# Attention, mixture of experts and FFN in one kernel: the products with v in plain float32, two heads side by side on TensorE's columns

## The chip, the cores and the metric

The kernel runs on one NeuronCore of one Trainium2 chip. The metric is the device time of one execution in microseconds (us). TensorE (PE) multiplies matrices and writes PSUM banks; VectorE (DVE), ScalarE (ACT) and GpSimd (POOL) do the elementwise work; the queue of SyncE (SP) starts nearly all DMA transfers. PSUM has eight banks here, each a tile of 128 partitions by 512 float32.

## The reference, cut to what matters

Three blocks follow one another on 4 batches of 448 rows. The first is causal attention with 12 heads of width 64, the second a layer of 4 experts, each of which is causal attention with one head of width 64 on the output of the first block, and the third an FFN with a convolution of three taps and a gate.

```
scores = scale * q @ k.T ; scores = where(mask, -1e9, scores)
attn = exp(scores - max) ; attn = attn / (sum(attn) + 1e-9)
x = attn @ v                                  # 12 heads, joined to 768 columns
for e in range(4):                            # experts: top 2 of 4 by x @ w_gate
    a = softmax(causal(scale * (x @ wq[e]) @ (x @ wk[e]).T))
    out += weight[e] * (a @ (x @ wv[e]) @ wo[e])
h = relu(out @ w_in) ; g = h * sigmoid(conv3(h)) ; y = g @ w_out
```

Everything is float32.

## The kernel before

Two heads make a pair. There are 24 pairs of attention (kind A, six for each batch) and 8 pairs of experts (kind M, two for each batch), so 64 heads. One head goes through these steps, each of which is a task with an engine:

- `score(i)`: PE, for four blocks of 112 rows (`CP`), two matmuls each. Operands are float32 numbers that have been split into a high and a low part of type float32r (`hi`, `lo`), so that a product is a sum of products of parts.
- `rowmax(i)` on DVE adds the mask and takes the maximum; `soft(i)` on ACT takes the exponential and the sum; `total`, `recip` on DVE; `norm(i)`, mostly on POOL, scales the rows of P.
- `transpose(g)`: PE turns P in three groups (448, 336 and 336 columns) into one of the two banks of kind `t`.
- `evac_hi(g)` copies a group out of the bank into `PT[:, 0]` as float32r (ACT; the six pairs of batch 0 are `plain`, and there ACT or DVE copies plain float32). `evac_lo(g)`, not for plain pairs, is a subtraction on DVE that reads the bank again and leaves the low part in `PT[:, 1]`. The bank is free after the last of the two.
- `pv(kts)`: PE multiplies with v. For a pair that isn't plain a head has two matmuls (high and low part of P) for each of four blocks of keys, 448, 336, 224 and 112 columns wide, against the weights `vhl[:, kt, 2h:2h+2]`, which hold the high part of v in 64 columns and the low part in the other 64. The two halves of the result are added by `out_corr` (ACT moves one half to `corr`) and `out_add` (DVE). For attention `x_hi` and `x_lo` on POOL then split x for the projections. For a plain pair a head has one float32 matmul for each block, with 64 columns of zeros beside v, and both heads sum into one bank, from which `pair_hi` and `pair_lo` split x at once.
- `v_hi`, `v_lo` on POOL split v of attention, `hi` and `lo` in `proj_v` that of the experts.

After a batch of attention come the projections `proj_qk` and `proj_v` for the experts; `fold_all` multiplies two weight matrices in the first 100 us. When all attention is done, `ffn_batch` and `ffn_out` do the FFN, with 1189 and 1257 as the lines of their matmuls.

No order is written out. `Program.run` is a planner: it walks through the program by a table of costs, and whenever an engine is idle it gives it the ready task of least priority number. The numbers are the table `PR` with one entry for each kind of task, `slot` for each pair. `ON` names the engines that may do a task. A task waits until the rings (`RINGS`, numbers of buffers) and the banks (`BANKS`) that it takes are free. Where the planner sees PE idle for more than 700 ns it puts in matmuls of `ident` with `ident` (`warm`, line 1334), whose results nobody reads. The order that it finds is fixed in the program; on the chip the engines only wait for each other.

Of the kernel before, what the change touches and what calls it, by code (L numbers as in the profile page):

```python
# [228 lines left out]
def attn_moe_ffn_kernel(  # L229
# [36 lines left out]
        P=3, PT=2, corr=2, x=2, nat=1, vn=1, skA=2, vhl=2, vw=2, skM=1, vhlm=1, wg=2,  # L266
# [4 lines left out]
        load=(-4152.0, 11493.0, -1929.0, 5893.5), prep=(-8501.0, 606.5, 168.5, 1518.0),  # L271
        vprep=(4890.5, 5076.0, 7982.5, 3170.0), wproj=-17.5, fold0=-467.0, fold=668.5,
        qk0=(-10900.5, -1866.5, -3202.0, 5747.5), v=(-554.5, -1155.5, -1893.5, 6792.5),
        qk1=(4984.5, 10288.0, 5857.0, 19987.0), evac=-3899.0, conv=-3380.0,
        wo=(-773.0, 5888.0, 4809.0, 9654.5, 9915.0, -4676.5), ffn0=-468.5,
        ffn=(5269.5, -4888.0, -1095.5, 4301.5), out=(2595.5, -1563.5, 2796.0, 1162.5),
        score=(2666.5, -704.5, 997.0, 78.5), rmax=(1169.5, 6674.0, 10054.0, -6359.0),
        exp=(2561.5, 12273.0, 3900.0, 4812.0), norm=(904.0, -404.5, -7099.5, 3076.5),
        tr=(4788.5, -3723.5, -5228.5, 1482.5), ev=(2394.5, 3956.5, -11469.5, -4991.0),
        pv=(5059.0, 512.0, -387.5, -3863.0), add=(-16794.0, 5422.5, -5662.5, -4891.0),  # L280
        x=(-1686.0, -6739.0, 4964.5, -45.5),
        slot=(-7300.5, -2095.0, -90.5, -898.5, 1247.5, 448.0, -4323.5, -2977.5, -2425.5, -1965.0, -9667.5, -1739.0, -466.5, -5300.0, 186.0, 145.5, -187.5, -146.5, 3848.5, 1960.5, 2151.5, -2484.5, 3906.0, 4302.5, 2325.0, 2446.5, 5199.0, 4478.5, 6267.0, 8256.0, 5325.5, -2013.5),
        other=(915.5, 3925.5, -1195.0, 6291.5, 8511.0, -4886.0, 7267.5, -2114.0, 1707.0, 15001.0, -10618.5, -9762.0, 1518.0, -1739.0, 5427.0, -14433.5, -6126.0),
        rows=(1435.0, 3384.5),
    )
    ON = dict(
        ql=('P', 'P', 'P', 'P'), norm=('PA', 'P', 'P', 'PD'), evp=('AD', 'A', 'A', 'A'), x_hi=('AP', 'P', 'P', 'P'),
        x_lo=('P', 'P', 'P', 'P'), v_hi=('P', 'P', 'P', 'P'), v_lo=('P', 'P', 'P', 'P'),
        q_hi=('DAP', 'A', 'A', 'A'), corr=('AD', 'A', 'A', 'A'), ev=('AD', 'A', 'A', 'A'),
        osb=('A', 'D', 'DA', 'A'),  # L290
    )
    KINDS = tuple(ON)
# [16 lines left out]
    def f(ap):  # L309
        return ap.bitcast(F32)  # L310
# [125 lines left out]
    for n, j in enumerate(order):  # L436
        j.slot = 8 * n
        j.slot += PR["slot"][n]
        j.plain = j.kind == "A" and j.b == 0
        j.phase = (0 if j.b == 0 else 1) if j.kind == "A" else 3 if j.b == B - 1 else 2  # L440
# [45 lines left out]
    def prep_twice(j):  # L486

        ready = {}
        for h in (1, 0):
# [3 lines left out]
            def load(h=h, st=st):  # L493
                if h == 1:
                    alloc_sk(j)
                t = pools["a"].tile([P, 2, TRI], F32, tag="PT", name=f"nat{h}", bufs=RINGS["PT"])
                st["nat"] = t[:, :, :S]
# [22 lines left out]
    def prep(j):  # L520
        n = f"{j.b}_{j.p}"
        nat, vn = Buf("nat"), Buf("vn")
        j.skb, j.vb = Buf("skA"), Buf("vhl")
# [5 lines left out]
        def load_v():  # L529
            j.v_nat = pools["head"].tile([CP, NQ, 2, D], F32, tag="vn", name=f"vn_{n}", bufs=1)  # L530
            nc.sync.dma_start(j.v_nat, v[j.b, j.p])
# [8 lines left out]

        def zero():
            j.vhl = pools["head"].tile([CP, NQ, 4, D], F32R, tag="vhl", name=f"vhl_{n}", bufs=RINGS["vhl"])
            nc.gpsimd.memset(f(j.vhl[:, :, 1, :]), 0.0)

        def load_v_apart():
            for h in range(2):
                nc.sync.dma_start(f(j.vhl[:, :, 2 * h]), v[j.b, j.p, :, :, h])
# [851 lines left out]
```

## Time and profile before

| | |
|---|---|
| time, median of 3 | 575.79 us (575.44 to 576.03) |
| the profiled execution | 573.99 us, of which its span is 572.2 us |
| PE busy | 94% of the span |
| DVE, ACT, POOL busy | 72%, 69%, 52% |
| mean granted TensorE clock | 0.979 of full speed |

The span goes from the first to the last instruction. A row of the profile names the line of the kernel, the engine, the operation, and the output and inputs by the program's names. A float32r matmul is one record; a plain float32 matmul is two (line 700 has 48 instructions and 96 records, line 1334 has 93 and 186).

### The profile page before, as it was taken

Reading aid. Unit: us, or ns where it says so; the run is one execution under the profiler, and the core shown is the slowest. Engines: PE = TensorE matmul, PEld = TensorE weight load, DVE = VectorE, ACT = ScalarE, POOL = GpSimd, SP = SyncE. Lnnn points to the kernel's source line nnn. Section 1 sums busy time; section 2 is a strip of 40 time slices with the busy share of each in tenths; the row PEclk is TensorE's granted clock in tenths of the full one; section 3 lists DMA queues with packets and bytes.
Section 4 is the critical chain, followed back from the end, with each engine's and each line's share of the span. In section 5 each row is a group of like instructions: output and inputs, shape, how many; then the busy total and the mean of one; then the engine's idle time right before and its main releaser. Section 6 shows DMA issues by size and latency. Waiting matters only on the chain.

```text
span 572.2 us, 10496 instructions
## 1 busy us (share of the span) xinstructions
PE 536.3 (94%) x3338; PEld 483.9 (85%) x3338; DVE 409.7 (72%) x1201; ACT 393.4 (69%) x1030; POOL 298.0 (52%) x466
## 2 busy tenths in 40 slices
PE   7979998899999999999989999978899999999997
PEld 7768787788988989888889999967798999889996
DVE  4879897785886888879867896588989962990000
ACT  3878768785896988989877996458758623881111
POOL 3465668686867779989679963444161330000000
PEclk8999999989999999999999999997999999999999
DMA  9998995787247376585665342161122131001111
GB/s 252 239 220 208 242 223 130 189 220 177 83 118 182 92 174 170 139 193 123 151 153 134 89 111 74 38 145 38 39 89 78 64 103 48 18 17 49 48 49 48
DMA packets 33287, 70.92 MB, mean 124 GB/s; under 512 B 9904, under 2 KB 18224, under 8 KB 33232
## 3 DMA queue, kind: packets, MB, share of 16 engines
q1 hardware_dynamic: 32944, 69.80, 47.9%
q10 hardware_dynamic: 288, 0.46, 0.3%
q8 instruction: 26, 0.43, 0.3%
q14 instruction: 29, 0.24, 0.1%
HBM read 32.74 MB, written 5.51 MB: 67 GB/s over the span
## 4 chain that ended last, share of the span: by engine, by line
PE 56%; DVE 19%; ACT 9%; DMA 8%; issue 4%; POOL 3%; SPq 1%; DVEq 0%; ACTq 0%; POOLq 0%
PE bank L1257 16%; PE bank L613 8%; PE bank L965 7%; PE bank L709 7%; PE bank L663 7%; PE bank L1011 5%; DVE bank L1210 4%; DMA sk_A<-sk_A 3%; PE bank L1189 2%; DMA nat<-in_qk_dram 2%; PE bank L700 2%; DVE PT_A L683 2%; DVE P_A L626 2%; ACT P_A L635 2%; ACT PT_A L319 1%
## 5 line engine op out<-in xcount | busy, mean ns | idle before, releaser
L1257 PE MATMUL bank<-g,wout 128*128 128x448 f32 x576 | 120.5, 367 | 0.0
L1257 PEld LDWEIGHTS bank<-g,wout 128*128 128x128 f32 x576 | 108.0, 188 | 9.7
L321 POOL TENSOR_SCALAR P_A<-P_A,r_A 112x448 f32<-112x448 f32 (+3 forms) x181 | 91.1, 518 | 37.5 <-DVE r_A L646 26.8
L635 ACT ACTIVATE P_A<-P_A,nm_A 112x448 f32<-112x448 f32 x192 | 100.2, 525 | 13.3 <-DVE nm_A L626 11.0
L613 PE MATMUL bank<-sk_A 128*112 128x112 f32 (+3 forms) x384 | 82.8, 326 | 10.7 <-DMA sk_A<-sk_A 5.7
L626 DVE CUSTOM_DVE_ANT_0 P_A<-bank,mask 112x448 f32<-112x448 f32 x192 | 81.7, 443 | 13.2 <-PE bank L613 12.1
L613 PEld LDWEIGHTS bank<-sk_A 128*112 128x112 f32 x384 | 57.3, 181 | 21.4 <-DVE nm_A L626 6.8
L663 PE MATMUL bank<-ident,P_A 112*112 112x112 f32 x480 | 66.7, 264 | 8.1 <-DVE PT_A L683 5.3
L965 PE MATMUL bank<-xT,wqk 128*128 128x448 f32 x288 | 73.5, 377 | 0.3 <-DVE wqk L941 0.2
L683 DVE TENSOR_TENSOR PT_A<-bank,PT_A 112x336 fp32r<-112x336 f32 (+1 forms) x108 | 57.9, 542 | 16.8 <-ACT PT_A L319 15.2
L319 ACT ACTIVATE PT_A<-bank 112x336 fp32r<-112x336 f32 (+2 forms) x128 | 59.5, 474 | 7.9 <-PE bank L663 6.9
L663 PEld LDWEIGHTS bank<-ident,P_A 112*112 112x112 f32 x480 | 49.5, 134 | 17.8 <-DVE PT_A L683 10.3
L328 POOL TENSOR_TENSOR sk_A<-nat,sk_A 128x896 fp32r<-128x896 f32 x23 | 48.5, 2109 | 19.5 <-ACT sk_A L319 12.0
L965 PEld LDWEIGHTS bank<-xT,wqk 128*128 128x128 f32 x288 | 49.7, 189 | 3.6 <-DVE wqk L941 1.0
L1189 PE MATMUL bank<-ocs,wp 128*128 128x448 f32 x192 | 45.8, 386 | 4.3 <-DVE g L1227 4.3
L709 PE MATMUL bank<-PT_A,vhl 112*128 112x448 f32 (+3 forms) x288 | 49.4, 316 | 0.0
L1210 DVE SCALAR_TENSOR_TENSOR bank<-h,cw,bank 128x448 f32<-128x448 f32 x64 | 43.0, 688 | 6.4 <-ACT bank L1208 5.7
L709 PEld LDWEIGHTS bank<-PT_A,vhl 112*128 112x128 f32 x288 | 46.2, 197 | 1.5
L1189 PEld LDWEIGHTS bank<-ocs,wp 128*128 128x128 f32 x192 | 37.1, 199 | 10.2 <-DVE g L1227 6.6
L319 ACT ACTIVATE osb<-bank 128x448 f32<-128x448 f32 x18 | 9.8, 545 | 47.1 <-PE bank L1257 47.0
L1011 PE MATMUL bank<-wvg,xT 128*112 128x260 f32 x288 | 41.4, 286 | 0.7 <-DVE sk_M L981 0.7
L321 POOL TENSOR_SCALAR P_M<-P_M,r_M,g_w 112x336 f32<-112x336 f32 (+3 forms) x60 | 34.1, 580 | 6.3 <-DVE r_M L646 4.8
(115 smaller groups left out, 1021.8 us busy)
## 6 DMA issues: line engine op xcount, KB each, us to landing
nat<-in_qk_dram SPq DMA_DIRECT2D x23, 448.0 KB, 5.1
sk_A<-sk_A SPq DMA_DIRECT2D x46, 224.0 KB, 4.3
sk_A<-sk_A SPq DMA_DIRECT2D x23, 336.0 KB, 3.4
wraw<-in_w_in_dram SPq DMA_DIRECT2D x12, 512.0 KB, 6.0
woraw<-in_w_out_dram SPq DMA_DIRECT2D x12, 512.0 KB, 3.8
out_dram<-osb SPq DMA_DIRECT2D x24, 224.0 KB, 1.9
sk_A<-sk_A SPq DMA_DIRECT2D x46, 112.0 KB, 4.0
vn<-in_v_dram SPq DMA_DIRECT2D x18, 224.0 KB, 4.0
```

The costliest lines, as they stand in the source:

```text
L319: nc.scalar.activation(dst, src, AF.Copy, scale=scale)
L321: nc.gpsimd.tensor_scalar(dst, src, scale, 1.0 if scale2 is None else scale2, ALU.mult, ALU.mult)
L613: nc.tensor.matmul(sp[:CP, :w], t[:, 1 - h, i * CP : (i + 1) * CP], t[:, 1 - h + k, :w], start=(k == 2), stop=(k == 1),)
L626: nc.vector.tensor_tensor_reduce(rows(i), st["s", i][:CP, :w], mask[:, S - w :], -SCALE, 3.0e38, ALU.add, ALU.min, st["nm"][:, i : i + 1],)
L635: nc.scalar.activation(rows(i), rows(i), AF.Exp, bias=st["nm"][:, i : i + 1], scale=-1.0, accum_out=st["sm"][:, i, 0:1],)
L663: nc.tensor.transpose(pt[:CP, o : o + CP], rows(i)[:, kt * CP : (kt + 1) * CP], ident[:CP, :CP])
L683: nc.vector.tensor_tensor(st["PT"][:, 1, b0 : b0 + w], pt, f(st["PT"][:, 0, b0 : b0 + w]), ALU.subtract)
L709: nc.tensor.matmul(st["ov"][:, kt * CP : S], j.vhl[:, kt, 2 * h : 2 * h + 2, :], st["PT"][:, s, col_base[kt] : col_base[kt] + w], start=(k ...
L965: nc.tensor.matmul(st["ps"][:, :S], proj["wqk"][:, a, cc, w, p * P : (p + 1) * P], xT[b, cc][:, b2, :], start=(cc == 0 and (a, b2) == PASS ...
L1011: nc.tensor.matmul(st[i][:CP, :VW], xT[b, cc][:, a, i * CP : (i + 1) * CP], proj["wvg"][:, b2, cc, :], start=(cc == 0 and (a, b2) == PASSE ...
L1189: nc.tensor.matmul(st["ps", c][:, :S], wp[:, a, ec, c * P : (c + 1) * P], st["oc"][:, b2, ec], start=(ec == 0 and (a, b2) == PASSES[0]), s ...
L1257: nc.tensor.matmul(st["ps"][:, :S], ffn["wout", n][:, a, c], gs[c][:, b2], start=(c == 0 and (a, b2) == PASSES[0]), stop=(c == NFC - 1 and ...
```

## The change

- v stays float32. It is loaded as it is (`load_v`, one DMA for each pair, in a ring of three), and the tasks `v_hi`, `v_lo`, `zero`, `load_v_apart` and the `lo` of `proj_v` are gone.
- P keeps no parts. `evac(g)` is one copy out of the bank, by ACT or DVE. The ring `PT` has four buffers of half the size, one for each head.
- `products_v` takes the place of `pv`, `out_corr`, `out_add`, `x_hi` and `x_lo`: when all six groups of a pair are copied, eight float32 matmuls with 64 columns of weights follow one another, head 1 and head 0 in turn. Head 1 writes partitions 64 to 127 of a bank, head 0 partitions 0 to 63. In the built program these are set as 128 by 64 tiles of the array at column 64 and column 0; all other matmuls are set as 128 by 128. An expert pair is then copied to `oc` at once, an attention pair is split from the bank into x (ACT or DVE, then DVE).
- FFN results have a ring of their own (`osb`, 4), and `oc` is split into two buffers, one for each pair of experts.
- The numbers in `PR` and the choices in `ON` are other ones.

```diff
-        PT=2, corr=2, x=2, nat=1, vn=1, skA=2, vhl=2, vhlm=1, ...
+        PT=4, osb=4, nat=1, skA=2, vn=3, vm=1, ...
-        score=(2666.5, -704.5, 997.0, 78.5), rmax=(1169.5, 6674.0, 10054.0, -6359.0),
+        score=(8996.0, -638.0, 1743.0, -7812.5), rmax=(-1352.5, 6783.0, 22485.0, -7290.0),
...
-        def evac_lo(g):
-            def go():
-                pt, b0, w = st["pt", g]
-                nc.vector.tensor_tensor(st["PT"][:, 1, b0 : b0 + w], pt, f(st["PT"][:, 0, b0 : b0 + w]), ALU.subtract)
...
-                    for s in range(2):
-                        nc.tensor.matmul(
-                            st["ov"][:, kt * CP : S],
-                            j.vhl[:, kt, 2 * h : 2 * h + 2, :],
-                            st["PT"][:, s, col_base[kt] : col_base[kt] + w],
...
+        cost = sum(2 * ((S - kt * CP) / 1.2 + PVX) for kt in range(NQ))
+        def pv():
+            st["ov"] = ps(vb)
+            for kt in range(NQ):
+                for h in (1, 0):
+                    nc.tensor.matmul(
+                        st["ov"][h * D : (h + 1) * D, kt * CP : S],
+                        j.v[:, kt, h, :],
+                        j.PT[h][:, col_base[kt] : col_base[kt] + S - kt * CP],
+                        start=(kt == 0),
+                        stop=(kt == NQ - 1),
+                    )
+        t = add("PE", prio + PR["pv"][j.phase], cost, pv, j.evs + j.vready, take=[vb], free=[j.PTb[1], j.PTb[0], j.vb])
...
+        def x_hi(e):
+            x = xT[(j.b, j.p)] = pools["x"].tile([P, 2, S], F32R, tag="xT", name=f"xT_{j.b}_{j.p}", bufs=RINGS["xT"])
+            copy(e, x[:, 0], st["ov"][:, :S])
+        def x_lo():
+            x = xT[(j.b, j.p)]
+            nc.vector.tensor_tensor(x[:, 1], st["ov"][:, :S], f(x[:, 0]), ALU.subtract)
```

The places in the order that matter are three. In the rows below a name carries the pair, the head and a running number (`PT_M_0_1_1867` is P transposed of the expert pair 0, head 1; since the change a further digit says whose head it is).

PE before, about two fifths into the attention: the products of two heads of an expert pair, scores of an attention pair between them.

```order
L709 MATMUL bank_65<-PT_M_0_1_1867,vhlm_1634 128x448 x2
L709 MATMUL bank_65<-PT_M_0_1_1867,vhlm_1634 128x336 x2
L709 MATMUL bank_65<-PT_M_0_1_1867,vhlm_1634 128x224 x2
L709 MATMUL bank_65<-PT_M_0_1_1867,vhlm_1634 128x112 x2
L613 MATMUL bank_62<-sk_A_4_1462 112x336 x2
L613 MATMUL bank_61<-sk_A_4_1462 112x224 x2
L709 MATMUL bank_66<-PT_M_0_0_1921,vhlm_1634 128x448 x2
```

PE of the change, the same pair.

```order
L581 MATMUL bank_61<-sk_A_4_1747 112x448 x2
L695 MATMUL bank_66<-PT_M_0_1_1_1884,vm_1579 64x448
L695 MATMUL bank_66<-PT_M_0_1_0_1885,vm_1579 64x448
L695 MATMUL bank_66<-PT_M_0_1_1_1884,vm_1579 64x336
L695 MATMUL bank_66<-PT_M_0_1_0_1885,vm_1579 64x336
L695 MATMUL bank_66<-PT_M_0_1_1_1884,vm_1579 64x224
L695 MATMUL bank_66<-PT_M_0_1_0_1885,vm_1579 64x224
L695 MATMUL bank_66<-PT_M_0_1_1_1884,vm_1579 64x112
L695 MATMUL bank_66<-PT_M_0_1_0_1885,vm_1579 64x112
L581 MATMUL bank_62<-sk_A_4_1747 112x336 x2
```

Two groups of eight float32r matmuls into two banks have become one group of eight float32 matmuls into one bank.

DVE before, at the same place: subtractions of P's low part (683) and sums of halves (726) between the maxima (626).

```order
L683 TENSOR_TENSOR PT_A_3_0_1808<-bank_64,PT_A_3_0_1808 112x336
L626 ISA P_A_4_1_1861,nm_A_4_1_1862<-bank_61,mask 112x448
L626 ISA nm_A_4_1_1862 112x1
L683 TENSOR_TENSOR PT_M_0_1_1867<-bank_63,PT_M_0_1_1867 112x448
L626 ISA P_A_4_1_1861,nm_A_4_1_1862<-bank_62,mask 112x336
...
L683 TENSOR_TENSOR PT_M_0_1_1867<-bank_64,PT_M_0_1_1867 112x336
L726 TENSOR_TENSOR x_A_3_1_1811<-bank_66,corr_A_3_1_1810 64x448
L683 TENSOR_TENSOR PT_M_0_1_1867<-bank_63,PT_M_0_1_1867 112x336
```

DVE of the change: copies (321) of some groups, each the only reader of its bank, and the low part of x straight from a bank (720).

```order
L321 TENSOR_SCALAR PT_M_0_1_1_1884<-bank_64 112x448
L321 TENSOR_SCALAR PT_M_0_1_1_1884<-bank_63 112x336
L896 TENSOR_TENSOR sk_M_1_1892<-bank_68,sk_M_1_1892 128x448
L611 TENSOR_REDUCE r_M_0_0_1821<-sm_90 112x4
L720 TENSOR_TENSOR xT_0_1912<-bank_65,xT_0_1912 128x448
```

On DVE 156 subtractions (683) and 52 sums (726) are gone; copies out of banks into `PT` are 94 where there were 16, and low parts of x (now line 720) are 24 where there were 6.

PE before, at the end of attention (1189 is the FFN's first product, 1334 the planner's matmuls of `ident`): the products of the last four heads stand behind the first product of the FFN, the last three of them here or below.

```order
L1334 MATMUL bank_65<-ident 128x128 x4
L709 MATMUL bank_66<-PT_M_0_0_5003,vhlm_4692 128x448 x2
...
L1334 MATMUL bank_62<-ident 128x128 x8
L1189 MATMUL bank_61<-ocs_4894,wp 128x448 x6
L1189 MATMUL bank_63<-ocs_4894,wp 128x448 x6
L1334 MATMUL bank_62<-ident 128x128 x6
...
L1334 MATMUL bank_62<-ident 128x128 x6
L663 MATMUL bank_64<-ident,P_M_1_1_4971 112x112 x3
L663 MATMUL bank_63<-ident,P_M_1_1_4971 112x112 x3
L1334 MATMUL bank_61<-ident 128x128 x3
```

PE of the change: one pair is left there, its products in one piece.

```order
L634 MATMUL bank_64<-ident,P_M_1_1_4436 112x112 x4
L1237 MATMUL bank_62<-ident 128x128 x5
L1096 MATMUL bank_61<-ocs_0_4363,wp 128x448 x3
...
L634 MATMUL bank_64<-ident,P_M_1_0_4479 112x112 x6
L1237 MATMUL bank_62<-ident 128x128 x8
L695 MATMUL bank_66<-PT_M_1_1_1_4542,vm_4156 64x448
L695 MATMUL bank_66<-PT_M_1_1_0_4543,vm_4156 64x448
```

The pair M_0 of the last batch is now finished before the FFN's first product. The planner puts 37 matmuls of `ident` between the last projection and the FFN's second product, where it had put 49; in the whole program 77, where there were 93.

## Rows read from the trace of the kernel before

**Rows 1.** The page, part 1: busy time and share of the span for each engine.

```profile
PE 536.3 (94%) x3338; PEld 483.9 (85%) x3338; DVE 409.7 (72%) x1201; ACT 393.4 (69%) x1030; POOL 298.0 (52%) x466
```

**Rows 2.** Busy time by stretch: length, PE, PEld, DVE, ACT, POOL, clock, DMA, GB/s.

```profile
0.00:25.00 25.00, 20.62 (x108) 17.55 (x109) 15.81 (x46) 14.33 (x35) 10.42 (x22) 0.93 0.96 250
25.00:100.00 75.00, 68.01 (x458) 58.26 (x457) 63.07 (x198) 59.04 (x166) 49.71 (x64) 0.98 0.84 205
150.00:370.00 220.00, 211.82 (x1506) 194.96 (x1505) 172.55 (x617) 181.85 (x529) 164.56 (x260) 1.00 0.53 126
370.00:420.00 50.00, 42.62 (x258) 38.56 (x257) 42.93 (x91) 34.01 (x74) 19.18 (x36) 0.90 0.24 64
420.00:510.00 90.00, 88.19 (x432) 79.69 (x431) 71.65 (x123) 56.86 (x109) 18.18 (x35) 1.00 0.20 66
510.00:572.00 62.00, 58.54 (x284) 52.84 (x282) 6.15 (x11) 10.65 (x20) 0.00 (x0) 1.00 0.12 45
```

**Rows 3.** The same for line 1334 alone: length, PE, PEld, clock, DMA, GB/s.

```profile
0.00:25.00 25.00, 10.99 (x56) 10.47 (x56) 0.93 0.96 250
370.00:420.00 50.00, 13.20 (x98) 12.40 (x98) 0.90 0.24 64
sum 572.00, PE 28.90 PEld 27.00; mean PE 4.13 PEld 3.86
```

**Rows 4.** The chain that ended last, products with v: start, us, what, records.

```profile
20.05 2.16 PE bank L700 x8
23.90 1.93 PE bank L700 x8
...
45.55 1.92 PE bank L700 x8
...
147.78 1.12 PE bank L709 x8
...
157.52 1.12 PE bank L709 x8
```

**Rows 5.** Groups by line on PE: count, busy us, mean ns of one, idle before.

```profile
L1257 PE MATMUL bank<-g,wout 128*128 128x448 f32 x576 | 120.5, 367 | 0.0
L700 PE MATMUL bank<-PT_A,vhl 112*128 112x448 f32 (+3 forms) x96 | 27.9, 414 | 0.0
```

**Rows 6.** What PE waited for: us in total, times, longest.

```profile
PE bank L613 <- DMA sk_A<-sk_A: 5.7, 4, 2.6
PE bank L663 <- DVE PT_A L683: 5.3, 11, 1.3
...
PE bank L663 <- ACT PT_A L319: 2.2, 1, 2.2
PE bank L663 <- DVE PT_M L683: 1.5, 3, 0.8
...
PE bank L663 <- DVE PT_A L325: 0.3, 1, 0.3
```

**Rows 7.** Groups by line on DVE: count, busy us, mean ns of one, idle before.

```profile
L683 DVE TENSOR_TENSOR PT_A<-bank,PT_A 112x336 fp32r<-112x336 f32 (+1 forms) x108 | 57.9, 542 | 16.8 <-ACT PT_A L319 15.2
L683 DVE TENSOR_TENSOR PT_M<-bank,PT_M 112x336 fp32r<-112x336 f32 (+1 forms) x48 | 25.3, 539 | 2.3 <-ACT PT_M L319 1.8
L726 DVE TENSOR_TENSOR x_A<-bank,corr_A 64x448 f32<-64x448 f32 x36 | 22.3, 621 | 6.8 <-ACT corr_A L319 5.9
L726 DVE TENSOR_TENSOR oc<-bank,corr_M 64x448 f32<-64x448 f32 x16 | 9.9, 620 | 2.5 <-ACT corr_M L319 2.2
L325 DVE TENSOR_SCALAR PT_A<-bank 112x336 f32<-112x336 f32 x11 | 5.4, 504 | 0.6 <-PE bank L663 0.6
```

**Rows 8.** Groups on DVE from 370 to 420 us alone.

```profile
L683 DVE TENSOR_TENSOR PT_M<-bank,PT_M 112x336 fp32r<-112x336 f32 x8 | 3.9, 504 | 0.1
L683 DVE TENSOR_TENSOR PT_M<-bank,PT_M 112x448 fp32r<-112x448 f32 x4 | 2.5, 620 | 0.9 <-ACT PT_M L319 0.9
L726 DVE TENSOR_TENSOR oc<-bank,corr_M 64x448 f32<-64x448 f32 x4 | 2.5, 618 | 0.1
```

More of the change, by code (lines that the diff above doesn't have):

```diff
@@ L594, in head @@
         st = {}
-        Pb, PTb, vb = Buf("P"), Buf("PT"), j.pb if j.plain else Buf("v")
+        Pb = Buf("P")
         ex, nm = {}, {}
@@ L748, in head @@
             nm[i] = add(eng, prio + PR["norm"][j.phase], 0, norm(i), [t] + gate, free=[j.wgb] if moe else [])
-        if j.plain:
-            take = [] if h == 0 else [vb]
-        else:
-            take = [vb] if h == 0 else [vb, corr] if moe else [vb, corr, xb]
-        first, last, evs = [], [], []
+        tr = None
         for g, kts in enumerate(GROUPS):
@@ L756, in head @@
             tb = st["tb", g] = Buf("t")
-            need = [nm[i] for i in range(min(kts), NQ)] + ([tr] if first else [])
-            t = tr = add("PE", prio + PR["tr"][j.phase], 98 * w / CP, transpose(g), need, take=[tb] if first else [tb, PTb], free=[Pb])
-            eng = either("evp" if j.plain else "ev", j.phase, {"ACT": act_ps(w), "DVE": dve(w)})
-            th = add(eng, prio + PR["ev"][j.phase], 0, evac_hi(g), [t] + first, free=[tb])
-            first = first or [th]
-            evs.append(th)
@@ L763, in head @@
-            if not j.plain:
-                evs.append(add("DVE", prio + PR["ev"][j.phase], dve(w), evac_lo(g), [th], free=[tb]))
-            for group in PVS[j.phase]:
-                if group[-1] not in kts:
-                    continue
-                cost = sum(4 * (S - kt * CP) / 2.4 if j.plain else mm(S - kt * CP, 2) for kt in group)
-                need = evs + j.vready + (last or j.first_pv)
-                t = add("PE", prio + PR["pv"][j.phase], cost, pv(group), need, take=[] if last else take, free=[PTb, j.vb])
-                if not last:
-                    j.first_pv = [t]
-                last = [t]
@@ L795, in head @@
-        if h == 0 and not moe and not j.plain:
-            def x_hi(e):
-                t = pools["x"].tile([P, 2, S], F32R, tag="xT", name=f"xT_{j.b}_{j.p}", bufs=RINGS["xT"])
-                xT[(j.b, j.p)] = t
-                copy(e, t[:, 0], j.dst)
-            def x_lo(e):
-                t = xT[(j.b, j.p)]
-                two(e, t[:, 1], j.dst, f(t[:, 0]), ALU.subtract)
-            eng = either("x_hi", j.phase, of_one(S))
-            th = add(eng, prio + PR["x"][j.phase], 0, x_hi, j.done, take=[xbuf[j.b, j.p]], free=[xb])
-            tl = add(either("x_lo", j.phase, of_two(S)), prio + PR["x"][j.phase], 0, x_lo, [th], free=[xb])
-            xdone[j.b, j.p] = [th, tl]
-            j.done = j.done + [th, tl]
+            need = [nm[i] for i in range(min(kts), NQ)] + [tr]
@@ new lines, in head @@
+            take = [tb] + ([j.PTb[1], j.PTb[0]] if h == 1 and g == 0 else [])
+            tr = add("PE", prio + PR["tr"][j.phase], 98 * w / CP, transpose(g), need, take=take, free=[Pb])
+            if g == 0:
+                if h == 1:
+                    j.first_tr = tr
+                else:
+                    j.first_tr.users.append(tr)
+                    tr.left += 1
+            eng = either("ev", j.phase, {"ACT": act_ps(w), "DVE": dve(w)})
+            j.evs.append(add(eng, prio + PR["ev"][j.phase], 0, evac(g), [tr], free=[tb]))
```

198 lines of the change are left out of this document (63 added, 135 removed).

## The prediction

> **What bounds the kernel now.** I read the busy times first: PE is busy for 536.3 of 572.2 us, DVE for 72%, ACT and POOL for less [rows 1]. The stretches come next, because an average over stages hides who waits. Between 150 and 370 us PE is busy for 211.8 of 220 us, with DVE at 172.6 and ACT at 181.9; from 420 to the end PE has 5.3 us of idle time in 152 [rows 2]. So PE sets the pace nearly everywhere, and a microsecond of PE work that goes is worth about one, unless something else is close behind. Not all of PE's busy time is work: 28.9 us are the planner's filler matmuls, 11.0 of them before 25 us and 13.2 between 370 and 420 us [rows 3]. With the 35.9 us in which PE is not busy (572.2 - 536.3) that makes 64.8 us without useful work. Two places hold most of it: the start (4.4 idle and 11.0 filled up to 25 us) and the passage from attention to the FFN (370 to 420 us: 7.4 idle and 13.2 filled, 20.6 of 50 us) [rows 2, 3]. There DVE is busy for 42.9 of 50 us, more than PE's useful 29.4. The list of waits says what PE stands still for elsewhere: 9.3 us before transposes (5.3 + 2.2 + 1.5 + 0.3), for a bank that DVE or ACT has yet to read out, and 5.7 us for the copies that DMA makes of q and k [rows 6].
>
> **Products with v on PE: what goes.** The chain shows a head's eight float32r records in 1.12 us, and a head's eight records in plain float32 in 1.92 to 2.16 us; I take 1.93 [rows 4]. There are 52 heads of the first kind (18 pairs of attention in batches 1 to 3 and 8 of experts) and 12 of the second (6 pairs): 52 x 1.12 + 12 x 1.93 = 81.4 us.
>
> **What comes.** 32 pairs, each with eight float32 matmuls of 448 to 112 columns, two of each width, so 16 records. The old plain head has the same eight records with weights of 128 columns instead of 64: 1.93 us for 2 x 1120 columns, 0.862 ns a column [rows 4]. No matmul in this trace shares the array with another, so whether head 1's and head 0's run side by side has to be bounded. At the one end they share perfectly and a pair costs what one head did: 1.93 us. At the other they don't share at all: 3.86 us. Between them is the order as it is written. The records stand as head 1 first pass, head 1 second pass, head 0 first pass, head 0 second pass, and so on for the next width. If PE starts them in this order, two of the same half can't overlap, and neighbours of different halves can. That gives nine steps, whose wider records have 448, 448, 448, 336, 336, 224, 224, 112 and 112 columns, 2688 in all: 2688 x 0.862 = 2.32 us. I take this, since it follows from the order in the program and a row. 32 x 2.32 = 74.2 us, so PE gains 81.4 - 74.2 = 7.2 us. The bounds are 61.8 us (a gain of 19.6) and 123.5 us (a loss of 42.1). The gain is not spread evenly: a plain pair falls from 3.86 to 2.32, 9.2 us over the six pairs of batch 0, while the other 26 pairs rise from 2.24 to 2.32, 2.1 us in all.
>
> What batch 0 gains isn't all kept. Up to 100 us the DMA engines are 0.96 and 0.84 busy [rows 2], and the copies of q and k that PE waits for (5.7 us [rows 6]) don't get shorter. The amount of v that is loaded is the same. I give back 3 us of the 9.2; the bounds are nothing and all of it.
>
> On the packing of narrow matmuls the Trainium skill ("TensorE: Matmul & The Clock Gate", Part 3: Packing small matmuls) reports 2.38 times the throughput for three column tiles of width 32. Scaled to two tiles, 1.59, an estimate from that page, a pair would take 3.86 / 1.59 = 2.43 us and PE would gain 3.6 us instead of 7.2. No row here shows two tiles at work.
>
> **DVE, ACT and POOL.** DVE loses 156 subtractions of 57.9 + 25.3 us and 52 sums of 22.3 + 9.9 us, 115.4 us in all [rows 7]. It gains 78 copies out of banks at 0.50 to 0.62 us (39 to 48 us), and 18 subtractions for x at 0.62 us, 11 us. Net some 60 of 410 us go. ACT loses 78 of its copies into PT and the moves to `corr`, and POOL the splitting of v and of attention's x. By themselves these are worth nothing, since neither engine is the bound; what counts is which of PE's waits they shorten. There are two.
>
> (a) The waits before transposes, 9.3 us [rows 6]. A bank used to be free after a copy on ACT and, after that, a subtraction on DVE (0.54 us in the mean [rows 7]) in its place in the queue between maxima. Now one read frees it. The transposes still need a bank of only two, and `PT` now holds two pairs until both heads' products are done, so a wait for the copy remains. Bounds: 0 and 9.3; I take half, 4.6 us.
>
> (b) The passage from attention to the FFN, 20.6 us without work. In this stretch 12 subtractions and 4 sums (3.9 + 2.5 + 2.5 = 8.9 us [rows 8]) leave the engine that is busiest there, and two copies (some 1.1 us) come. The last chain also gets shorter: subtraction and sum (0.5 and 0.6 us) and the move between them fall out of each head's way to the FFN. In the new order one pair instead of two is left behind the FFN's first product, and 12 fewer fillers stand there; a filler costs 13.2 / 49 = 0.27 us [rows 3], 3.2 us. Bounds: 0 and 8.9; I take 5 us. The FFN that follows has the same instructions, with PE busy for 146.7 of 152 us [rows 2], so it hands on what it gets.
>
> The start I put at zero. 33 fillers stand before the first product with v where 28 stood, but that product now serves both heads; x needs no other work than before.
>
> **The sum.** 574.0 us, the profiled execution, - 7.2 (products) + 3.0 (given back in batch 0) - 4.6 (transposes) - 5.0 (the passage) = 560.2. That execution was 0.3% below the median of the runs shown (573.99 to 575.79), so the median should be 560.2 x 1.0031 = 562 us, 2.4% faster.
>
> **Rivals.**
>
> - *No sharing.* Head 1's and head 0's matmuls run one after the other, 3.86 us a pair, and all 64 heads now cost what plain ones did. Places: 26 pairs lose 1.62 us each, where PE is busy for 96% of the time. 574.0 + 42.1 - 9.6 = 606, as a median 608 us. For it: no row shows sharing. Against it: each half has columns, weights and partitions of its own. The break-even lies at 2.54 + 9.6 / 32 = 2.84 us a pair without anything given back, so slower begins when less than two thirds of the step from 3.86 to 2.32 us comes.
> - *The array runs empty at each change of tile.* A record of line 1257 lasts 367 ns, but 576 take 120.5 us, 209 ns each [rows 5]: 158 ns of one lie under the next. If nothing may lie under the next one when PE goes from 128 columns to 64 and back, 64 changes cost 10.1 us. 562 + 10 = 572 us. The Trainium skill ("TensorEngine Tiling (Array Packing)", Key Properties) states that a change of tiling mode drains TensorE; it gives no price, and no row here has such a change. For it: 32 pairs scattered over the attention, each between scores or transposes. Against it no row speaks; it may also come in part.
> - *The waits move.* The products of a pair now need six copies of two heads instead of three or four of one, and the new order puts more copies on DVE between its maxima. If the transposes wait as long as before, and the passage too, 574.0 - 7.2 + 3.0 = 569.8, a median of 572 us.
> - *More than forecast.* The waits before transposes go entirely, the passage gains 8.9, and nothing is given back: 574.0 - 7.2 - 9.3 - 8.9 = 548.6, a median of 550 us. For it: with 60 us less on DVE there is room at 150 to 370 us, where DVE, ACT and POOL are busy for 172, 182 and 165 of 220 us [rows 2].
>
> **How the numbers follow.** The forecast with its own range of 554 to 570 us has a chance of 0.50; more than forecast, 0.12; changes of tile or moved waits, 570 to 580 us, 0.20 together; no sharing, 0.14; another loss above 580 us by the new order, 0.04. The predicted time is that of the likeliest, 562. The range runs from 548 to 580 and leaves out no sharing, the other loss and the tail of the better case. A measurement of this kernel can tell about 0.2%, 1.2 us: its three runs lie within 0.6 us. Of the 0.20 between 570 and 580 I count 0.13 as faster, 0.03 as the same and 0.04 as slower. Faster: 0.50 + 0.12 + 0.13 = 0.75; same 0.03; slower 0.04 + 0.14 + 0.04 = 0.22.
>
> **What would show it.** The chain or the timeline should have a pair's 16 records in 2.2 to 2.5 us; near 3.9 means no sharing, near 2.6 a price of the change of tile, with idle time just before the first record or just behind the last. The waits of transposes for copies should sum to under 6 us. From the last projection to the FFN's second product idle and filled time should be near 15 us, and DVE's busy time near 350 us. Up to 100 us PE should show more idle time than now. The forecast would be wrong if the pair costs over 2.84 us, or if PE's idle and filled time, 64.8 us now, doesn't fall.

## The result, and the profile after

The changed kernel takes 554.45 us (median of 4, 552.43 to 556.19), beside 575.62 us (572.15 to 576.03) for the kernel before on the same chip: a ratio of 0.964 with a 95% interval of 0.959 to 0.970, 3.6% faster. The profiled execution took 555.16 us, with a span of 553.4 us at a mean granted clock of 0.981. The forecast was 562 us, with a range of 548 to 580.

The page of the changed kernel, part 1, answers to [rows 1].

```profile
PE 517.9 (94%) x3306; PEld 439.3 (79%) x3306; DVE 348.1 (63%) x1081; ACT 348.2 (63%) x931; POOL 226.5 (41%) x375
```

PE has lost 18.4 us of busy time, the span 18.8 us. DVE has lost 61.6 us, where the forecast had some 60. The stretches of the changed kernel follow (length, PE, PEld, DVE, ACT, POOL, clock, DMA, GB/s, as in [rows 2]; attention ends some 20 us earlier now, so the passage lies between 345 and 400 us).

```profile
0.00:25.00 25.00, 19.99 (x110) 17.40 (x112) 13.74 (x43) 14.66 (x34) 7.01 (x18) 0.86 0.87 245
25.00:100.00 75.00, 64.67 (x471) 52.59 (x468) 63.01 (x199) 64.35 (x182) 46.05 (x49) 0.98 0.85 215
...
150.00:345.00 195.00, 187.31 (x1337) 153.02 (x1337) 120.02 (x485) 129.91 (x396) 105.99 (x185) 0.98 0.57 136
345.00:400.00 55.00, 48.63 (x316) 41.18 (x310) 43.32 (x109) 38.54 (x92) 24.32 (x45) 0.97 0.32 88
400.00:490.00 90.00, 89.14 (x445) 81.13 (x442) 67.75 (x116) 52.64 (x102) 16.16 (x35) 1.00 0.16 52
```

The planner's matmuls of `ident` alone (line 1237 now) answer to [rows 3]; after the length the columns are PE, PEld, clock, DMA and GB/s.

```profile
0.00:25.00 25.00, 11.64 (x66) 11.15 (x66) 0.86 0.87 245
...
345.00:400.00 55.00, 8.16 (x62) 7.61 (x62) 0.97 0.32 88
...
sum 553.00, PE 23.58 PEld 21.97; mean PE 3.37 PEld 3.14
```

Together the two views split the 18.8 us that the span has lost. PE is idle for 35.5 us (553.4 - 517.9), 0.4 less than before; its filled time fell from 28.9 to 23.6 us, 5.3; and its useful work from 507.4 to 494.3 us, 13.1. In the passage idle time (6.4) and filled time (8.2) make 14.5 us of 55, where they were 20.6 of 50. Up to 25 us they make 16.6 us (15.4 before), and from 25 to 100 us PE is idle for 10.3 us (7.0 before).

The chain of waits of the changed kernel shows a pair's products (start, us, what, records).

```profile
24.29 2.06 PE bank L695 x16
94.67 2.04 PE bank L695 x16
...
211.37 2.44 PE bank L695 x16
...
324.12 2.04 PE bank L695 x16
```

All the pairs that this chain holds take 2.04 to 2.06 us, but for the one at 211.37 us. The single records of a pair in the trace show why it isn't the forecast's 2.32. The starts, in us after the first, with the widths in columns:

```
start  0 .007  .427 .434  .803 .810  1.085 1.092  1.368 1.375  1.557 1.564  1.746 1.753  1.842 1.849
width  448     448        336        336          224          224          112          112
next instruction of PE: 2.038
```

The records start in twos, 7 ns apart, so there are eight steps and not nine. The trace doesn't name the head of a record, but in run 1 below, where head 1 starts alone, its records have the same starts (0, .427, .803, 1.085, 1.368); so the two of a step are one of each head, and head 1's second pass doesn't hold up head 0's first. From the first start to the next instruction's it is 2.037 to 2.039 us in 28 of 32 pairs, and in one the records fell out of step and took 2.354 us; in the other three the granted clock or a wait of the next instruction lengthens it (2.44 to 3.34 us).

The groups by line of the changed kernel on PE and DVE (count, busy us, mean ns of one, idle before) answer to [rows 5, 7]: line 695 holds the products, 321 DVE's copies out of banks, 720 the low part of x.

```profile
L695 PE MATMUL bank<-PT_A,v 112*64 112x448 f32 (+3 forms) x384 | 51.3, 408 | 0.0
...
L321 DVE TENSOR_SCALAR PT_A<-bank 112x448 f32<-112x448 f32 (+1 forms) x71 | 38.8, 556 | 11.4 <-PE bank L634 9.9 <-ACT P_M L603 0.8
...
L695 PE MATMUL bank<-PT_M,vm 112*64 112x448 f32 (+3 forms) x128 | 16.9, 406 | 0.0
L720 DVE TENSOR_TENSOR xT<-bank,xT 128x448 fp32r<-128x448 f32 x24 | 14.8, 617 | 5.9 <-ACT xT L315 5.7
```

The busy times of the products now, 51.3 + 16.9 = 68.2 us, can't be set beside the forecast's 81.4 (before) and 74.2 (now), since records of neighbouring groups overlap in them. In the kernel before the same sum is 98.3 us (27.9 [rows 5] and two groups more):

```profile
L709 PE MATMUL bank<-PT_A,vhl 112*128 112x448 f32 (+3 forms) x288 | 49.4, 316 | 0.0
...
L709 PE MATMUL bank<-PT_M,vhlm 112*128 112x448 f32 (+3 forms) x128 | 21.0, 306 | 0.0
```

What can be compared with the forecast is the time from each record's start to the next record's, without idle time. By that the products took 84.5 us before and take 66.1 us now, 18.4 less. Before, most of the 52 heads took 1.10 to 1.19 us and not 1.12, and two of them, at the lower granted clock, 2.04 and 2.07 us.

What PE waited for in the changed kernel (us in total, times, longest) answers to [rows 6]; scores are line 581, transposes 634, maxima 594.

```profile
PE bank L581 <- DMA sk_A<-sk_A: 10.4, 9, 2.5
PE bank L581 <- DVE nm_M L594: 5.7, 7, 2.7
PE bank L581 <- DVE nm_A L594: 3.6, 8, 1.1
...
PE bank L634 <- ACT PT_A L315: 1.6, 3, 0.9
...
PE bank L634 <- ACT PT_M L315: 0.8, 2, 0.6
...
PE bank L634 <- DVE PT_M L321: 0.2, 1, 0.2
```

The waits before transposes fell from 9.3 to 2.6 us. The waits of scores for the DMA copies of q and k rose from 5.7 to 10.4 us, and those for maxima (5.7 + 3.6 = 9.3 us now) from 6.2:

```profile
PE bank L613 <- DVE nm_M L626: 3.6, 3, 2.7
PE bank L613 <- DVE nm_A L626: 2.6, 6, 0.5
```

The passage can be taken by the same two instructions in every run, from the last projection's last matmul to the first of the FFN's second product. It lasted 44.9 us before (372.6 to 417.6 us) and 38.0 us now (363.5 to 401.5): 6.9 of the 18.8 us.

### The profile page after: what moved, and what is told of

It reads as the page before. It is cut to its first block, busy times and chain, and to the rows that moved or that the text cites. A ratio compares the mean times of both kernels' runs of the same rounds, so it can differ in the third digit from the quotient of the medians.

```text
span 553.4 us, 10183 instructions
## 1 busy us (share of the span) xinstructions
PE 517.9 (94%) x3306; PEld 439.3 (79%) x3306; DVE 348.1 (63%) x1081; ACT 348.2 (63%) x931; POOL 226.5 (41%) x375
## 4 chain that ended last, share of the span: by engine, by line
PE 61%; DMA 14%; DVE 11%; POOL 5%; ACT 4%; issue 3%; SPq 3%; POOLq 0%; ACTq 0%; DVEq 0%
PE bank L1160 18%; PE bank L880 10%; PE bank L581 10%; PE bank L634 7%; DMA sk_A<-sk_A 7%; PE bank L695 7%; DMA nat<-in_qk_dram 4%; PE bank L1096 4%; PE bank L926 4%; DVE bank L1117 3%; POOL sk_A L324 3%; SPq L467 2%; DMA woraw<-in_w_out_dram 2%; DVE g L1134 1%; DVE P_A L594 1%
## 5 line engine op out<-in xcount | busy, mean ns | idle before, releaser
L317 POOL TENSOR_SCALAR P_A<-P_A,r_A 112x336 f32<-112x336 f32 (+3 forms) x169 | 83.6, 513 | 67.0 <-DVE r_A L614 43.9
L581 PE MATMUL bank<-sk_A 128*112 128x112 f32 (+3 forms) x384 | 81.9, 324 | 17.7 <-DMA sk_A<-sk_A 10.4
L634 PE MATMUL bank<-ident,P_A 112*112 112x112 f32 x480 | 64.8, 265 | 2.1 <-ACT PT_A L315 1.6
L634 PEld LDWEIGHTS bank<-ident,P_A 112*112 112x112 f32 x480 | 51.2, 135 | 7.2 <-POOL P_A L317 1.1
L695 PE MATMUL bank<-PT_A,v 112*64 112x448 f32 (+3 forms) x384 | 51.3, 408 | 0.0
L1096 PE MATMUL bank<-ocs,wp 128*128 128x448 f32 x192 | 43.9, 376 | 2.8 <-DVE g L1134 2.0
L321 DVE TENSOR_SCALAR PT_A<-bank 112x448 f32<-112x448 f32 (+1 forms) x71 | 38.8, 556 | 11.4 <-PE bank L634 9.9
L695 PEld LDWEIGHTS bank<-PT_A,v 112*64 112x64 f32 x384 | 25.8, 137 | 24.6 <-issue 13.9
L926 PE MATMUL bank<-wvg,xT 128*112 128x260 f32 x288 | 45.2, 293 | 0.1
L315 ACT ACTIVATE PT_A<-bank 112x336 f32<-112x336 f32 (+1 forms) x73 | 32.8, 464 | 17.9 <-PE bank L634 13.9
L317 POOL TENSOR_SCALAR P_M<-P_M,r_M,g_w 112x448 f32<-112x448 f32 (+3 forms) x58 | 33.2, 584 | 23.0 <-DVE r_M L614 15.0
```

The lines of the kernel that those rows point to most:

```text
L317: nc.gpsimd.tensor_scalar(dst, src, scale, 1.0 if scale2 is None else scale2, ALU.mult, ALU.mult)
L581: nc.tensor.matmul(sp[:CP, :w], t[:, 1 - h, i * CP : (i + 1) * CP], t[:, 1 - h + k, :w], start=(k == 2), stop=(k == 1),)
L634: nc.tensor.transpose(pt[:CP, o : o + CP], rows(i)[:, kt * CP : (kt + 1) * CP], ident[:CP, :CP])
L695: nc.tensor.matmul(st["ov"][h * D : (h + 1) * D, kt * CP : S], j.v[:, kt, h, :], j.PT[h][:, col_base[kt] : col_base[kt] + S - kt * CP], st ...
L926: nc.tensor.matmul(st[i][:CP, :VW], xT[b, cc][:, a, i * CP : (i + 1) * CP], proj["wvg"][:, b2, cc, :], start=(cc == 0 and (a, b2) == PASSE ...
L1096: nc.tensor.matmul(st["ps", c][:, :S], wp[:, a, ec, c * P : (c + 1) * P], st["oc", ec][:, b2], start=(ec == 0 and (a, b2) == PASSES[0]), s ...
```

## The experiments

Each run is the changed kernel with one edit, where nothing else is said. The ratio is to the kernel before, run beside it.

| run | time, us | ratio (95%) |
|---|---|---|
| the change | 554.45 | 0.964 (0.959 to 0.970) |
| 1 heads apart | 577.13 | 1.005 (1.002 to 1.008) |
| 2 six matmuls ahead of a pair, changing tiles | 589.90 | 1.026 (1.021 to 1.031) |
| 3 the same six, in two blocks | 571.76 | 0.994 (0.991 to 0.997) |
| 4 second read of each bank | 601.95 | 1.046 (1.043 to 1.050) |
| 5 the same load without the bank | 609.14 | 1.062 (1.055 to 1.069) |
| 6 second read in the passage alone | 561.11 | 0.977 (0.973 to 0.982) |
| 7 before, without the second read | 567.88 | 0.989 (0.985 to 0.993) |
| 8 before's priorities | 566.29 | 0.986 (0.981 to 0.991) |
| 9 to 11 other orders (costs 38, 46, 60) | 560.34, 558.72, 555.70 | 0.978, 0.974, 0.969 |

**1. Heads apart.** The two loops of `products_v` change places, so that head 1's four matmuls come before head 0's.

```diff
-            for kt in range(NQ):
-                for h in (1, 0):
+            for h in (1, 0):
+                for kt in range(NQ):
```

> The changed kernel with the two loops of the products with v exchanged: all four widths of head 1, then all four of head 0. Same instructions, same planned costs, so the same order of everything else. Theory (the two halves of the array work at once only where matmuls of the two halves stand next to each other): a pair's 16 records take about 3.9 us where they take 2.04 now, 32 pairs lose 1.8 us each, 58 us, and the time is near 612 us. Rival (PE looks far enough ahead to overlap them in any order): 2.0 to 2.1 us a pair and 554 us. A third way, that the gain of the change is not in the products at all but in the other engines: the pair gets slower and the time still stays below 575 us.

It took 577.13 us, 22.7 more, where 58 had been expected. The chain of this run has each pair in two pieces (start, us, what, records).

```profile
97.37 2.03 PE bank L695 x8
99.48 1.30 PE bank L695 x6
```

By the single records a pair now lasts 3.405 us in all 32 cases. Head 0's first record starts 1.374 us after head 1's, when head 1's fifth record has just started, and only four narrow ones (224, 224, 112 and 112 columns) lie beside others. So sharing isn't a matter of the halves alone: it needs matmuls of different halves close to each other in the program's order. Head 0's first record does start ahead of head 1's fourth matmul (1.746 and 1.842 us), but only when head 1's third has started. The 32 pairs cost PE 43 us more (32 x 3.405 = 109.0 against some 66, which is 32 x 2.04 and a little for the longer ones), but the time rose by 22.7. The page and the waits of this run show where a part of the rest is.

```profile
PE 555.6 (96%) x3306; PEld 460.6 (80%) x3306; DVE 347.5 (60%) x1081; ACT 349.2 (61%) x931; POOL 226.3 (39%) x375
```

```profile
PE bank L581 <- DVE nm_A L594: 3.4, 7, 1.4
PE bank L581 <- DMA sk_A<-sk_A: 2.7, 5, 1.6
...
PE bank L581 <- DVE nm_M L594: 1.9, 5, 0.5
```

PE's busy time rose by 37.7 us, since the other matmuls took some 5 us less (the mean granted clock was 0.985 instead of 0.981, which is a part of it), and its idle time fell by 15.0 (35.5 to 20.5): the waits for DMA fell from 10.4 to 2.7 us, those for an expert pair's maxima from 5.7 to 1.9. A slower PE hides what it had waited for. A microsecond of PE in the products is worth about half of one here.

**2 and 3. What a change of tile costs.** Both runs put six float32 matmuls of 32 columns ahead of each pair's products, into the free columns of the pair's bank. In run 2 they alternate between 64 and 128 columns of weights; in run 3 the same six stand in two blocks, so that a group of them has six changes less.

```diff
+            for m in (64, 128, 64, 128, 64, 128):     # run 3: (128, 128, 128, 64, 64, 64)
+                nc.tensor.matmul(st["ov"][:m, S : S + 32], ident[:, :m], ident[:, :32], start=True, stop=True)
```

> The changed kernel with six small float32 matmuls of 32 columns ahead of each pair's products, into unused columns of the same bank, alternating between 64 and 128 columns of the array, so that a pair has 8 changes of tile instead of 2. To be read against the next kernel, which has the same six matmuls in another order and 2 changes. If a change costs about 0.1 us, as the gaps around the products with v in the trace suggest (0.11 us ahead, 0.10 behind), the 6 x 32 = 192 more changes cost 19 us; if the array has to run empty for 0.158 us, 30 us; if changes are free, the two kernels agree within 1 us.

> The same six small matmuls ahead of each pair's products, first the three on 128 columns, then the three on 64, so that a pair has 2 changes of tile as in the changed kernel. Its time above the changed kernel's 554 us is what the 12 records themselves cost: between 0.04 and 0.1 us a record, 15 to 38 us in all. The difference to the kernel before this one in the list is the price of 192 changes of tile: 19 us by the theory, 30 us by the draining rival, 0 if they are free.

They took 589.90 and 571.76 us, 18.1 us apart, 94 ns for each of the 192 changes. The starts of the single records, in ns after the first, show the price directly (a matmul has two records):

```
run 3, 128 columns:       139 251 363 474             112 apart
run 3, 128 then 64:       474 680                     206
run 3, 64 columns:        759 818 876 934             59 apart
run 2, 128 then 64:       364 570,  934 1140          206
run 2, 64 then 128:        79 232,  649 802           153
run 2, first, second:       0  79,  570 649            79   (64 columns, just behind a change)
run 2, first, second:     232 364,  802 934           132   (128 columns, just behind a change)
```

206 instead of 112 in one direction and 153 instead of 59 in the other: 94 ns each way from record to record. Behind a change the matmul's own second pass comes 20 ns later too, after 79 ns instead of 59 and 132 instead of 112. So a change costs 114 ns here: the six narrow matmuls of run 2 take 1.710 us up to the first product, and 6 x 59 + 6 x 112 = 1026 ns would be theirs without the six changes. The agreement of 94 ns with the difference of the times is luck, since run 1 says that PE's time counts only in part, and in run 3 the narrow matmuls leave the two heads out of step, so that its products take some 2.24 us and not 2.04. By 94 to 114 ns the 64 changes of the changed kernel cost PE 6.0 to 7.3 us, where the rival had 10.1. The Trainium skill ("TensorEngine Tiling (Array Packing)", Key Properties) states that a change of tiling mode drains TensorE; the runs agree that a change costs something, and the price is theirs.

**4 and 5. What the second read cost.** Run 4 gives DVE the 156 subtractions back, which read a bank a second time, into a tile that nobody uses. Run 5 has the same number on a constant in SBUF, so that no bank is held. The order of the changed kernel stays.

```diff
                 copy(e, j.PT[h][:, b0 : b0 + w], pt)
+                if j.b or moe:
+                    nc.vector.tensor_tensor(junk[:, :w], pt, j.PT[h][:, b0 : b0 + w], ALU.subtract)   # run 4
+                    nc.vector.tensor_tensor(junk[:, :w], mask[:, :w], mask[:, :w], ALU.subtract)      # run 5
```

> The changed kernel with the 156 subtractions on DVE put back (outside batch 0), each reading the bank of transposes after the copy, so that the bank is held for two reads again and DVE has some 84 us more to do; their results go to a tile that nobody reads. Everything else keeps its order. Theory (one read instead of two is worth the waits before transposes, 9.3 us before and under 3 us after, and part of the passage to the FFN): these waits come back and the time rises by 6 to 14 us, to 560 to 568 us. Rival (the gain is in the products on PE alone, the other engines had room): within 2 us of 554 us.

> The changed kernel with 156 subtractions of the same sizes put on DVE at the same places as in the kernel with the second read, but on a constant in SBUF, so that DVE has about as much more to do and no bank is held for them, nor do they wait for ACT's copy. Order of the rest as in the changed kernel; results go to a tile that nobody reads. The second read took 601.95 us, 47.5 above the changed kernel. Theory (what costs is that a bank of transposes is held until DVE comes round): most of the 47 us go away, 565 to 575 us. Rival (DVE's load itself costs, by the maxima that come late): 585 to 600 us.

They took 601.95 and 609.14 us, far above either theory. PE's waits in run 4 (lines from 365 on stand one to three further; `junk` is the subtraction's output):

```profile
PE bank L635 <- DVE junk L646: 21.0, 47, 1.1
PE bank L582 <- DVE nm_A L595: 11.0, 20, 2.6
PE bank L582 <- DVE nm_M L595: 5.2, 11, 1.5
```

And in run 5:

```profile
PE bank L582 <- DVE nm_A L595: 21.5, 27, 3.1
PE bank L582 <- DVE nm_M L595: 8.8, 8, 2.6
...
PE bank L635 <- DVE PT_A L321: 2.7, 6, 0.6
PE bank L635 <- ACT PT_A L315: 2.6, 2, 2.3
...
PE bank L635 <- DVE PT_M L321: 1.9, 2, 1.6
...
PE bank L635 <- ACT PT_M L315: 0.7, 2, 0.5
```

In run 4 the transposes wait for the bank (21.0 us) and the scores for maxima that come late (16.2 us). In run 5 the first wait has shrunk to 7.9 us, for copies alone, and the second has grown to 30.3 us. So the held bank, as I had it, isn't needed for a cost of this size: a load on DVE does it without, 113 us in run 5, between the maxima in an order that was made without it (POOL is a little slower there too, and makes 3.0 us of PE's waits). How much of run 4's 47.5 us the held bank makes isn't shown, since run 5 loads DVE with 28 us more (the section on the hardware has the rows). Nor do the waits make up the whole of either cost: PE's idle time rose by 25.4 and 29.9 us, and its busy time by 21.9 and 24.6 with the same matmuls. A lower granted clock (0.976 and 0.965 instead of 0.981) is a part of that; the rest isn't traced.

**6. The passage alone.** The subtraction of run 4 only for the two expert pairs of the last batch, 12 in all.

```diff
+                if moe and j.b == B - 1:
+                    nc.vector.tensor_tensor(junk[:, :w], pt, j.PT[h][:, b0 : b0 + w], ALU.subtract)
```

> The changed kernel with its order kept; for the two expert pairs of the last batch alone, DVE also reads each group back out of the bank by a subtraction into a tile that nobody uses: 12 instructions. With all 156 a group cost 0.545 us in the mean, so 12 are some 6.5 us of DVE, in the stretch in which DVE is the busiest engine and PE is filled or idle for 14.5 us. Theory (in the passage DVE sets the end, as the forecast's 5 us for the passage assumes): +3 to +6.5 us, 557.5 to 561 us, and idle and filled time of PE between 345 and 400 us up from 14.5 to some 18 to 21. Rival (the passage is bound by a chain of small steps, and its gain came from the new order): under +1.5 us, at most 556 us.

It took 561.11 us, 6.7 more, in the median of 6. The group of the subtractions from 340 to 410 us, the stretch with the passage, and the matmuls of `ident` in it:

```profile
L646 DVE TENSOR_TENSOR junk<-bank,PT_M 112x336 f32<-112x336 f32 (+1 forms) x12 | 6.5, 542 | 1.0 <-ACT PT_M L315 0.9
```

```profile
345.00:407.00 62.00, 52.97 (x328) 43.27 (x325) 50.11 (x123) 40.12 (x95) 24.45 (x45) 0.94 0.28 80
```

```profile
345.00:407.00 62.00, 9.32 (x72) 8.77 (x73) 0.94 0.28 80
```

6.5 us of DVE cost 6.7 us of time. From the last projection to the FFN's second product the run took 43.1 us (364.1 to 407.2) instead of 38.0, so 5.1 us come in the passage. In the stretch shown idle and filled time make 9.0 + 9.3 = 18.4 us, 3.8 more than in the changed kernel. Over the whole span idle time rose by 3.6 us, filled time by 0.5 and useful work by 2.6; in the passage the granted clock fell from 0.97 to 0.94, which may be a part of the 5.1 us. There a microsecond of DVE is worth 0.8 (5.1 of 6.5 us): for the most part DVE sets its end.

**7. The kernel before without the second read.** In the kernel before the 156 subtractions are left out, and the products take the high part of P a second time in place of the low part, so that PE does the same work; the low part's share of the result is missing. Its order stays.

```diff
-                nc.vector.tensor_tensor(st["PT"][:, 1, b0 : b0 + w], pt, f(st["PT"][:, 0, b0 : b0 + w]), ALU.subtract)
...
-                            st["PT"][:, s, col_base[kt] : col_base[kt] + w],
+                            st["PT"][:, 0, col_base[kt] : col_base[kt] + w],
```

> The kernel before with the 156 subtractions on DVE left out and nothing else moved: the order of all that is left is the old one, and PE does the same matmuls, where the high part of P stands in for the low part (so the low part of P is missing from the result). It shows what the missing second read is worth by itself, without the new products and the new order. Theory: the waits of transposes for copies (9.3 us) shrink to about 3 and some waits of scores for maxima go, 4 to 10 us faster than before, 566 to 571 us. Rival (PE sets the pace, so only its products count): within 2 us of the kernel before. Rival (it is nearly all of the gain): 558 us or less.

It took 567.88 us where the kernel before took 573.95 beside it, 6.1 us less. Its waits of PE (scores are line 613 and transposes 663, as in [rows 6]):

```profile
PE bank L613 <- DMA sk_A<-sk_A: 11.2, 8, 2.7
...
PE bank L663 <- ACT PT_A L319: 3.1, 4, 1.4
...
PE bank L663 <- DVE g L1226: 1.0, 1, 1.0
...
PE bank L663 <- DVE PT_A L325: 0.3, 1, 0.3
```

The waits of transposes fell from 9.3 to 4.4 us, and those for the copies of q and k rose from 5.7 to 11.2: a PE that isn't held up arrives at the DMA's copies early. So what was won before the transposes was lost again there. The passage, from the last projection to the FFN's second product, took 41.7 us (371.0 to 412.7) instead of 44.9. These 3.2 us are the larger part of the 5.2 us between the two profiled spans, and nearly half of the 6.9 us that the change wins in the passage.

**8. The changed kernel with the priorities of the kernel before.** `PR` has its old numbers (for tasks that are new, those of the nearest old task); the planner then puts in 93 matmuls of `ident` instead of 77.

```diff
-        score=(8996.0, -638.0, 1743.0, -7812.5), rmax=(-1352.5, 6783.0, 22485.0, -7290.0),
...
+        score=(2666.5, -704.5, 997.0, 78.5), rmax=(1169.5, 6674.0, 10054.0, -6359.0),
...
```

> The changed kernel with the table of priority numbers of the kernel before, wherever an entry has a counterpart (the copies out of the banks take that of the plain pairs, the copy of x that of the old move); engines, rings, banks and instructions stay those of the changed kernel. The planner then puts in 93 matmuls of ident where it puts 77. Theory (the products and the missing second read make the gain, the new search adds some us): 556 to 570 us. Rival (the new search makes most of it): 570 us and more, no faster than the kernel before.

It took 566.29 us: still 1.4% faster than before, and 11.8 us slower than the changed kernel. These numbers had been found for another program, so 11.8 is what the search gave over numbers that don't fit; it isn't a clean share of the gain.

**9 to 11. Other orders.** One cost of the planner's table is changed, the fixed one of a product with v (`PVX = 55`), to 38, 46 or 60. The work is the same but for the matmuls of `ident` (80, 83 and 84 of them); the order changes, and which engine makes some of the copies.

```diff
-    PVX = 55
+    PVX = 38     # 46, 60
```

> The changed kernel with the planner's cost for a pair's products set to 2.17 us (the constant 55 in it made 38), near the 2.04 us from first to next record and the gap ahead of it that the trace shows, where the planner had 2.31. Instructions and numbers are the same, only the order found is another. A look at how much an order found by chance is worth: between 552 and 570 us; below 552 would be a better kernel, and 80 matmuls of ident instead of 77 speak for slightly above 554.

> The changed kernel with one number of the planner's table changed, the fixed cost of a matmul with v (55 to 46), so that another order of the same instructions comes out, with 83 matmuls of ident in the program instead of 77. The same edit to 38 cost 6 us. If the numbers searched for with 55 are worth something beside the program itself, any other order is slower: 557 to 563 us. If orders scatter evenly about the measured one, 551 to 558 us.

> As the run with 46, the fixed cost 60 instead of 55, 84 matmuls of ident: 557 to 563 us if the search is worth something, 551 to 558 us if orders scatter evenly.

They took 560.34, 558.72 and 555.70 us. The best can't be told from the changed kernel, and none beats it; of the last two, one fits that the search is worth something and the other that orders scatter evenly. One lucky order is worth up to 6 us here, and 3.8 over the mean of the three.

## Why the prediction was right

By its own steps:

- **Products with v: right in kind, too small.** The forecast took 2.32 us a pair by nine steps, 74.2 us in all, a gain of 7.2. The two heads run in eight steps of twos, 2.04 us, and from start to start the products went from 84.5 to 66.1 us, 18.4 less. The step ahead of each pair, which the record before it bears, takes back 32 x 0.094 = 3.0 us; PE's useful work as a whole fell by 13.1 us, so some 2 us more went elsewhere, which isn't traced. The premise that led to the wrong size is "If PE starts them in this order": each half goes on by itself, and the other head's record doesn't wait for its turn. The kernel before was put too low as well, 81.4 for 84.5 us. The estimate by the Trainium skill ("TensorE: Matmul & The Clock Gate", Part 3: Packing small matmuls), 2.43 us a pair, was further off than the one from the row. Run 1 shows that the price hangs on the order of the matmuls.
- **Changes of tile: the rival was right that they cost, and its price was too high.** 94 to 114 ns and not 158, 6.0 to 7.3 us and not 10.1. The forecast had them at nothing; eight steps instead of nine saved more, 32 x 0.28 = 9.0 us.
- **A microsecond of PE is worth about one: wrong.** Run 1 gives 22.7 us of time for 43 us of PE. Waits that PE hides when it is slow come out when it is fast, first the DMA copies of q and k. So the 13.1 us of work need not have given 13.1 us of time by themselves; how many they gave can't be read from a sum in which the waits move too. That idle and filled time came out near the forecast (5.7 us less, forecast 6.6) is partly luck: the waits before transposes fell by more and others rose.
- **Given back in batch 0: right in kind.** Forecast 3.0; from 25 to 100 us PE's idle time rose by 3.3 us, and the waits for copies of q and k rose by 4.7 over the whole span.
- **Waits before transposes: right, larger.** Forecast 4.6 less, measured 6.7 less (9.3 to 2.6). Run 7 shows the cause: the same waits shrink, to 4.4 us, when only the second read goes. But scores now wait 9.3 us for maxima, where it was 6.2, which takes part of it back; the rival *The waits move* had this mechanism at another place.
- **The passage: right.** Forecast 5.0, measured 6.1 of idle and filled time (20.6 to 14.5 us). Run 6 shows that DVE sets the end there for the most part, and run 7 that the second read makes 3.2 of the 6.9 us by which the passage is shorter, in the old order and by itself.
- **The start: nearly.** Put at zero, it lost 1.2 us.
- **"By themselves these are worth nothing" (the relief of DVE, ACT and POOL): right only for an order made for the load.** In the order of the kernel before, 83.2 us of subtractions cost 6.1 us (run 7); put into an order that doesn't know of them, 85 us cost 47.5 (run 4). That it is the order that makes the difference is argued and not shown: DVE's busy time is 422 us in run 4 and 410 in the kernel before.
- **The order.** The forecast gave the new numbers a value only through the passage. The changed kernel and runs 8 to 11 show orders of the same work from 554 to 566 us. That is as large as any term of the sum, and no row of the kernel before could have priced it.

Useful work came out 5.9 us better than forecast (13.1 against 7.2), idle and filled time 0.9 worse (5.7 against 6.6). The time is inside the range, at the lower end of the forecast's own 554 to 570 us, because of the products, from which the better case expected nothing more. That is 5.0 us of the 7.6 between forecast and measurement. The rest is within the noise, which the forecast put too low: it said 1.2 us, and the four runs of each kernel spread over 3.8 to 3.9 us.

What stays open is how the 21 us divide between PE's shorter products, DVE's relief and the search: the runs give 22.7 us for sharing, 6.1 for the second read in the old order and 11.8 for the numbers, and these overlap.

## What to carry to other kernels

A sum over one engine prices work, not time: where DMA or another engine waits close behind, undo the saving alone and see how much of it comes back (here half). The place of a load decides its price more than its length: 6.5 us of DVE put into the passage cost 6.7 us, while 83 us in an order laid out for them cost 6. Where two small matmuls are to share the array, write them next to each other; and where a search sets the order, measure some neighbours before a difference of 1% is put down to the change.

## What the runs showed of the hardware

- Two float32 matmuls with 64 columns of weights each, on the two halves of the columns and next to each other in the order, start 7 ns apart and run side by side through both their passes: 2.04 us a pair, where one head with 128 columns took 1.93 [rows 4]. With four of the same half in front of the other four, the second half starts with the third of the first, and the pair takes 3.405 us.
- Going from 128 columns to 64 or back costs 94 ns each way from record to record, and 20 ns more before the second pass of the matmul behind it (runs 2 and 3).
- A DVE subtraction with one operand from a bank took 545 ns in run 4, one with both from SBUF 725 ns in run 5; POOL's scaling of P rose from 513 to 554 ns at the same time. The groups of run 5 (count, busy us, mean ns of one):

```profile
L646 DVE TENSOR_TENSOR junk<-mask 112x448 f32<-112x448 f32 (+1 forms) x156 | 113.1, 725 | 0.8
L317 POOL TENSOR_SCALAR P_A<-P_A,r_A 112x336 f32<-112x336 f32 (+3 forms) x169 | 90.7, 554 | 105.5 <-DVE r_A L615 89.8 <-ACT P_A L604 4.9 <-DVE PT_A L321 4.2
```

The 28 us that run 5 loads DVE with beyond run 4 come from there. What the two engines share isn't shown by these runs.
